# Moving weight conversion, stage A, a fold and an evacuation between the ticks of a Fourier and two-layer-pair kernel

## The chip, the cores and the metric

The kernel runs on one core of one Trainium2 chip. The metric is device time in microseconds (us), median of several executions. Five engines work beside each other, each through its own queue in program order: TensorE (PE; its weight loads are listed as PEld), VectorE (DVE), ScalarE (ACT), GpSimd (POOL) and SyncE (SP, which only issues DMAs). An instruction that waits holds up all that stands behind it in its own queue.

## The reference

```
X   = fft(fft(x, axis=1), axis=2).real        # x: 2 x 3008 x 256
h   = X.reshape(6016, 256) @ w_in             # 256 x 2048
g   = where(h > 0, h, exp(min(h, 0)) - 1)
y   = g @ w_out                               # 2048 x 256
h2  = y @ w2_in
g2  = max(h2, 0) + alpha * min(h2, 0)
out = g2 @ w2_out
```

All four weight matrices arrive as 64 bit floats and are turned into 32 bit floats on the chip.

## The kernel before, in words

**Precision.** A matmul operand is kept as a pair hi + lo of the PE's faster 32 bit type. A product takes three matmuls: w hi by x hi, w lo by x hi, w hi by x lo (`PASSES`, L465). ACT writes hi (a copy that rounds), and POOL or DVE subtracts to get lo.

**Stages.** Stage A is the first transform (L181), stage B the second (L277); the third is folded into w_in (`w_fold`, L376). Then come 96 *ticks* of the first layer pair (L598) and 48 *pairs* of the second (L705). A tick t belongs to one block of 512 (or 452) tokens and one slice f of 128 of the 2048 hidden features. Blocks and slices come in the order of `SEGS` (L42): ticks 0 to 7 are block 0 with f 0 to 7, ticks 8 to 15 block 1 with f 0 to 7, ticks 16 to 23 block 0 with f 8 to 15, ticks 24 to 31 block 1 with f 8 to 15, and from tick 32 on one block each 16 ticks.

**One tick** puts its instructions out in this order: hooks *pre*; gemm1(t) on PE (6 matmuls, L477); pt (L610) and ht (L614) on DVE; hi of tick t-2 on ACT (L589); hooks *mid*; where the segment of t-3 ends, its gemm2 and the evacuation of half of the accumulators by DVE (L513); ReLU and exp on ACT (L630, L636, and from tick 42 on L641 into PSUM); lo of t-2 on POOL (L595); the combination of t-1 on DVE (L582, L579); where a segment ended, the other half of its accumulators by ACT (L511); hooks *end*; and last gemm2(t-3) on PE (12 matmuls, L493). So gemm2(16) is the last thing of tick 19, and gemm2(20) of tick 23. PE is about one tick ahead of ACT and POOL. Segments end so that the evacuations lie in ticks 10, 18, 26, 34, 50, 66 and 82.

**Weights.** A conversion of a matrix part takes an ACT copy (`conv_y`, L338) and three DVE steps (`conv_s`: L356, L358, L360). Then `w_split` (L412) makes hi on ACT (L435) and lo on POOL (L436) for one half of the part: half 0 serves two slices f, half 1 the next two. w_out part 2 serves f 8 to 11, part 3 serves f 12 to 15. The hooks of these are set by tables: `CONV1` (part, tick of the copy, ticks of the three steps, ticks of the two splits), `STAGE_A1` (where the two halves of each chunk of the second batch's stage A stand), `FOLD`, and `KEEP` for the second layer's weights (load, copy; steps at +0, +2, +4). All are registered at L822 to L899. `at_split` puts a split among the *end* hooks of its tick.

**Start.** Before tick 0 stage B of block 0 runs with half a part of w_out converted beside it (L297 to L307): the DVE steps stand between the subtractions that make the low part of stage B's output, which `hold` keeps back and `release` puts out.

The PSUM of gemm1 has four banks that go round; from tick 42 on it has two, and exp takes the other two.

Of the kernel before, what the change touches and what calls it, by code (L numbers as in the profile page):

```python
# [43 lines left out]
E_PSUM = 42  # L44
# [8 lines left out]
CONV1 = [  # L53
    (('i', 1, 2), 8, (8, 9, 11), ()),
    (('i', 1, 3), 11, (12, 13, 14), ()),
    (('o', 1, 2), 14, (14, 15, 16), (17, 18)),
    (('o', 1, 3), 18, (18, 20, 21), (21, 22)),
]

STAGE_A1 = [  # L60
    (0, (7, 'pre'), (8, 'pre')), (1, (9, 'pre'), (11, 'pre')), (2, (12, 'pre'), (14, 'pre')), (3, (16, 'pre'), (17, 'pre')),
]
LOAD_X = {3: 9}
FOLD = {2: (13, 'pre', 0), 3: (15, 'mid', 0)}
LOAD_V = {(0, 2): 12, (1, 0): 24, (1, 1): 24, (1, 2): 24}
STAGE_B = {(0, 1): 5, (0, 2): 22, (1, 2): 32, (1, 0): 36, (1, 1): 40}
LOAD_ZB = {1: 6, 2: 29, 3: 45, 4: 61, 5: 77}
# [2 lines left out]

KEEP = [
    (("i", 2, 0), 31, 34, 81),
    (("o", 2, 0), 36, 39, 84),
    (("i", 2, 1), 45, 48, 88),
    (("o", 2, 1), 52, 55, 92),
    (("i", 2, 2), 59, 61, 95),
# [1 line left out]
]  # L78
FINAL_1 = [(84, "i", 0, 0), (86, "i", 0, 1), (88, "o", 0, 0), (90, "o", 0, 1), (92, "i", 1, 0), (94, "i", 1, 1)]
DIRECT = {("o", 2, 2): 95, ("o", 2, 3): 0}  # L80
PREP_0 = [("x", 62), ("t3", 64, 65), ("t1", 67, 68), ("b11", None, 69), ("t2", 74, 75), ("b21", None, 76), ("t4", 78, 82),
          ("b22", None, 83)]
FIRST = [
# [21 lines left out]
def tile_fft_moe_elu_moe_prelu(  # L105
# [171 lines left out]
    def stage_b(b, g):  # L277
        v = vt.pop((b, g))
        bl = BL[b, g]
        z = big.tile([128, 2, 2, 512], F32R, tag="big", name="zt")  # L280
        for q in range(2):
            p = mmtile()
            for k in range(4 * q, 4 * q + 4):
                o = p.rearrange("p (e k n) -> p e k n", e=2, k=4)[:, :, k % 4, :]
                mm(out=o, lhsT=v[:, k, 0:128], rhs=r64_sb[:, 0:128], start=True, stop=False)
                mm(out=o, lhsT=v[:, k, 128:256], rhs=r64_sb[:, 128:256], start=False, stop=True)
            pv = p.rearrange("p (e m) -> p e m", e=2)
            own = BLOCKS[bl][2] - (MOVED if bl == LONG else 0)
            m = min(256, own - q * 256)
            cuts = [(z, q * 256, 0, m)]  # L290
            if q == 1 and bl == SHORT:
                cuts.append((moved, 0, m, m + MOVED))
            for to, c0, m0, m1 in cuts:
                hi = to[:, 0, :, c0:c0 + m1 - m0]
                act(out=hi, in_=pv[:, :, m0:m1], func=ACTF.Copy)
                hold(("b", b, g, q), tt, out=to[:, 1, :, c0:c0 + m1 - m0], in0=pv[:, :, m0:m1], in1=hi.bitcast(F32), op=ALU.subtract)
            if b == g == 0:  # L297
                if q == 0:
                    release("b", b, g, 0)
                    delta_0(v)  # L300
                    conv_y("o", 1, 0, 0)
                else:
                    spread_0()
                    conv_s("o", 1, 0, 0, 0)
                    release("b", b, g, 1)
                    conv_s("o", 1, 0, 0, 1)
                    conv_s("o", 1, 0, 0, 2)  # L307
        if bl == LONG:
            hold(("b", b, g, 1), nc.gpsimd.tensor_copy, out=z[:, :, :, BLOCKS[bl][2] - MOVED:BLOCKS[bl][2]], in_=moved.bitcast(F32))
        zt[bl] = z  # L310
# [40 lines left out]
    def conv_s(kind, layer, c, i, step):  # L351

        t, y = words((kind, layer, c), i)
        hi, y = t[:, :, 1], y.bitcast(I32)
        if step == 0:
            nc.vector.tensor_scalar(out=hi, in0=hi, scalar1=-(1 << 31), scalar2=None, op0=ALU.bitwise_and)  # L356
        elif step == 1:
            stt(out=hi, in0=t[:, :, 0], scalar=29, in1=hi, op0=ALU.logical_shift_right, op1=ALU.bitwise_or)  # L358
        else:
            stt(out=y, in0=y, scalar=3, in1=hi, op0=ALU.logical_shift_left, op1=ALU.bitwise_or)  # L360
# [8 lines left out]
    def hold(key, fn, *a, **kw):  # L369
        held.setdefault(key, []).append(lambda: fn(*a, **kw))  # L370

    def release(*key):
        for fn in held.pop(key):
            fn()
# [121 lines left out]
    def evac(L, bl, f, first, last, ts, ds=(0, 1)):  # L496
        n = BLOCKS[bl][2]
        ac = accs[L, bl]
        if L == 1 and bl not in xs:
            xs[bl] = big.tile([128, 2, 2, 512], F32, tag="big", name="xs")  # L500
        for t in ts:
            for d in ds:
                if L == 1:
                    o = xs[bl][:, d, t, 0:n]
                else:
                    ot = wk.tile([128, 512], F32, tag="s", name="ot", bufs=4)
                    o = ot[:, 0:n]
                if first > 0:
                    tt(out=o, in0=ac[d][t][:, 0:n], in1=xs[bl][:, d, t, 0:n], op=ALU.add)
                elif t == 1:  # L510
                    act(out=o, in_=ac[d][t][:, 0:n], func=ACTF.Copy)  # L511
                else:
                    nc.vector.tensor_copy(out=o, in_=ac[d][t][:, 0:n])  # L513
                if L == 2:
                    for g, a, c0, m in pieces(bl):
                        nc.sync.dma_start(out=out[d * 128:(d + 1) * 128, c0 + t * BLK_N[g]:c0 + t * BLK_N[g] + m],
                                          in_=o[:, a:a + m])
            if L == 1 and last == NFT - 1 and 1 in ds:
                nc.sync.dma_start(out=xd[bl][:, :, t, 0:n], in_=xs[bl][:, :, t, 0:n])
# [48 lines left out]
    ticks = [(1, bl, f, f0, f1 - 1) for bl, f0, f1 in SEGS for f in range(f0, f1)]  # L568
    NT = len(ticks)
    LAG = 3  # L570

    def parts(t):
        return (slice(0, 1), slice(1, 2)) if t == 0 else (slice(0, 2),)
# [24 lines left out]
    def tick(t, pre, mid, end):  # L598
        cur = ticks[t] if t < NT else None
        for fn in pre:  # L600
            fn()
        if cur:
            L, bl, f = cur[:3]
            n = BLOCKS[bl][2]
            p = gemm1(bl, f, t >= E_PSUM)
            ht = wk.tile([128, 2, 512], F32, tag="h", name="ht")
            et = wk.tile([128, 2, 512], F32, tag="e", name="et", bufs=3)
            st[t] = dict(n=n, f=f, h=ht[:, :, 0:n], e=et[:, :, 0:n])
            pt = wk.tile([128, 512], F32, tag="s", name="pt", bufs=4)
            stt(out=pt[:, 0:n], in0=zb[bl][:, 0:n], scalar=an_sb[:, f:f + 1], in1=p[0], op0=ALU.mult, op1=ALU.add)  # L610
            for i, op in enumerate((ALU.add, ALU.subtract)):
                if t == 1:
                    combine(0, parts(0)[i:i + 1])
                tt(out=ht[:, i, 0:n], in0=pt[:, 0:n], in1=p[1], op=op)  # L614
        if t == 1:
            split_hi(0)
            split_lo(0)
        if t - 2 in st and t > 3:
            split_hi(t - 2)
        for fn in mid:  # L620
            fn()
        over = t < NT and t - LAG in st and ticks[t - LAG][2] == ticks[t - LAG][4]
        if over:
            s = st.pop(t - LAG)
            gemm2(*ticks[t - LAG], s["hi"], s["lo"])
            evac(*ticks[t - LAG], (0,))
        if cur:
            s = st[t]
            for i in parts(t):
                act(out=s["e"][:, i], in_=s["h"][:, i], func=ACTF.Relu, scale=-1.0)  # L630
                if t == 2:
                    combine(1)
                    split_hi(1)
                    split_lo(1)
                if t < E_PSUM or t == NT - 1:
                    act(out=s["e"][:, i], in_=s["e"][:, i], func=ACTF.Exp, scale=-1.0)  # L636
            if E_PSUM <= t < NT - 1:
                s["x"] = []
                for i in range(2):
                    s["x"].append(ps.tile([128, 512], F32, tag="ee", name="eet", bufs=2)[:, 0:s["n"]])  # L640
                    act(out=s["x"][i], in_=s["e"][:, i, :], func=ACTF.Exp, scale=-1.0)  # L641
        if t - 2 in st and t > 3:
            split_lo(t - 2)
        if t - 1 in st and t > 2:
            combine(t - 1)
        if over:
            evac(*ticks[t - LAG], (1,))
        for fn in end:
            fn()
        u = {2: 0, 3: None}.get(t, t - LAG)  # L650
        if u in st and t < NT:
            last_1(u)
# [138 lines left out]
    with tc.manual_schedule():  # L791
# [45 lines left out]
        at(9, load, ("o", 1, 2))  # L837
        for c, (t, where, n) in FOLD.items():
            at(t, w_fold, c, where=where)
# [48 lines left out]
        for bl in range(2, NBLK):  # L888
            for i, (pre, mid) in enumerate(AHEAD):
                for where, todo in (("pre", pre), ("mid", mid)):  # L890
                    for what, *args in todo:
                        at2(bl * NFT // 2 - len(AHEAD) + i, does[what], bl, *args, where=where)
        for name, t, *cs in PREP_0:
            if name == "x":
# [95 lines left out]
```

## Time and profile before

| | |
|---|---|
| median of 3 runs | 959.3 us (958.94 to 959.51) |
| the profiled execution's own time | 959.1 us |
| its span, first to last instruction | 957.3 us |
| mean granted TensorE clock | 0.999 |
| PE busy | 945.2 us, 99% of the span |
| DVE, ACT, POOL busy | 716.1, 654.3, 627.4 us |

The span is what lies between the first and the last instruction of the program; the time is 1.8 us longer. A busy PE counts a matmul from its start to a modelled end, so that short waits between two matmuls can hide in it. In a timeline row the bracket gives the idle time of that engine before the row, and what ended it.

### The profile page before, as it was taken

What the parts mean: (1) busy time and instruction counts of PE and PEld (TensorE: products, weight loads), DVE (VectorE), ACT (ScalarE), POOL (GpSimd) and SP (SyncE); (2) the same over time, 40 slices, a digit from 0 to 9 for tenths busy, and PEclk for the clock granted to TensorE, in tenths of its full rate; (3) what the DMA queues carried; (4) which work ended last, traced back from release to release, by engine and by line L of the source; (5) the groups of instructions that cost most, each with busy time, mean ns of one, the idle gap of its engine ahead of it and who ended that gap; (6) DMA issues with size and microseconds to landing.
All of it is one profiled execution on the core that took longest, in us unless ns stands there. A gap on an engine that the chain in (4) does not pass through costs nothing.

```text
span 957.3 us, 12202 instructions
## 1 busy us (share of the span) xinstructions
PE 945.2 (99%) x4206; PEld 768.5 (80%) x4206; DVE 716.1 (75%) x1015; ACT 654.3 (68%) x915; POOL 627.4 (66%) x495
## 2 busy tenths in 40 slices
PE   9999999999999999999999999999999999999998
PEld 3677678799888877888888888889988888888886
DVE  2899899989999998887787675565666567566564
ACT  5778777767788887888765665656566566565553
POOL 1366578755968779987878855647565664664543
PEclk9999999999999999999999999999999999999999
DMA  8966222311322210130230110020020011001001
GB/s 326 321 187 161 58 78 88 100 49 41 100 84 98 90 45 34 45 110 22 69 130 1 39 45 0 7 83 1 1 73 10 0 45 45 1 1 45 0 1 45
DMA packets 27189, 64.10 MB, mean 67 GB/s; under 512 B 3124, under 2 KB 11572, under 8 KB 25080
## 3 DMA queue, kind: packets, MB, share of 16 engines
q1 hardware_dynamic: 25696, 62.09, 19.6%
q10 hardware_dynamic: 1176, 1.07, 0.3%
q8 instruction: 33, 0.54, 0.2%
q0 software_dynamic: 256, 0.17, 0.1%
q14 instruction: 28, 0.23, 0.1%
HBM read 41.53 MB, written 21.79 MB: 66 GB/s over the span
## 4 chain that ended last, share of the span: by engine, by line
PE 83%; DVE 10%; issue 2%; ACT 2%; POOL 1%; ACTq 0%; DVEq 0%; POOLq 0%
PE acc L493 45%; PE eet L672 13%; PE mmt L672 10%; PE mmt L477 7%; DVE ht L614 2%; DVE et L582 2%; PE eet L477 2%; DVE pt L610 2%; PE mmt L187 1%; DVE w L358 1%; POOL lo L595 1%; DVE et L579 1%; DVE w L360 1%; PE eet L381 1%; ACT et L630 1%
## 5 line engine op out<-in xcount | busy, mean ns | idle before, releaser
L493 PE MATMUL acc<-hi,wo 128*128 128x512 f32 (+1 forms) x1536 | 429.4, 386 | 2.8 <-ACT hi L589 1.5
L698 POOL TENSOR_TENSOR lo<-et,hi 128x512 fp32r<-128x512 f32 (+1 forms) x190 | 237.6, 1281 | 180.8 <-ACT hi L692 180.8
L595 POOL TENSOR_TENSOR lo<-et,hi 128x512 fp32r<-128x512 f32 (+1 forms) x192 | 276.3, 1461 | 94.4 <-ACT hi L589 48.9
L493 PEld LDWEIGHTS acc<-hi,wo 128*128 128x128 f32 x1536 | 287.9, 188 | 59.5 <-ACT xs L511 2.2
L493 PE MATMUL acc<-lo,wo 128*128 128x512 f32 (+1 forms) x768 | 258.4, 387 | 1.0 <-POOL lo L595 1.0
L692 ACT ACTIVATE hi<-et 128x1024 fp32r<-128x1024 f32 (+1 forms) x96 | 100.3, 1045 | 132.2 <-PE acc L493 69.9
L493 PEld LDWEIGHTS acc<-lo,wo 128*128 128x128 f32 x768 | 143.3, 188 | 30.9 <-POOL lo L595 3.9
L630 ACT ACTIVATE et<-ht 128x1024 f32<-128x1024 f32 (+2 forms) x97 | 100.3, 1034 | 64.0 <-DVE ht L614 62.2
L724 DVE TENSOR_TENSOR v<-mmt,p 128x512 f32<-128x512 f32 (+1 forms) x48 | 32.7, 680 | 143.0 <-ACT p L719 142.8
L477 PE MATMUL mmt<-zt,wi 128*128 128x512 f32 (+1 forms) x438 | 113.1, 391 | 0.8 <-DVE ht L614 0.4
L589 ACT ACTIVATE hi<-et 128x1024 fp32r<-128x1024 f32 (+2 forms) x97 | 99.4, 1024 | 5.5 <-DVE et L582 4.1
L614 DVE TENSOR_TENSOR ht<-pt,mmt 128x512 f32<-128x512 f32 (+1 forms) x148 | 93.8, 675 | 8.0 <-DVE pt L610 0.5
L477 PEld LDWEIGHTS mmt<-zt,wi 128*128 128x128 f32 x438 | 81.8, 188 | 19.9 <-issue 1.5
L749 ACT ACTIVATE et<-mmt 128x512 f32<-128x512 f32 (+1 forms) x96 | 55.8, 589 | 28.9 <-PE mmt L672 14.6
L582 DVE SCALAR_TENSOR_TENSOR et<-et,ht 128x1024 f32<-128x1024 f32 (+2 forms) x44 | 67.1, 1525 | 1.4 <-POOL lo L595 1.1
L610 DVE SCALAR_TENSOR_TENSOR pt<-zb,an_sb,mmt 128x512 f32<-128x512 f32 (+1 forms) x72 | 52.7, 731 | 20.0 <-PE mmt L477 19.9
L579 DVE SCALAR_TENSOR_TENSOR et<-eet,ht 128x512 f32<-128x512 f32 (+1 forms) x106 | 67.1, 675 | 0.0
L752 DVE SCALAR_TENSOR_TENSOR et<-et,oma_sb,eet 128x512 f32<-128x512 f32 (+1 forms) x96 | 66.1, 730 | 0.0
L752 DVE SCALAR_TENSOR_TENSOR et<-et,oma_sb,mmt 128x512 f32<-128x512 f32 (+1 forms) x96 | 66.0, 729 | 0.0
L641 ACT ACTIVATE eet<-et 128x512 f32<-128x512 f32 (+1 forms) x106 | 58.9, 588 | 3.7 <-DVE et L579 2.1
L672 PE MATMUL eet<-xo,wi 128*128 128x512 f32 (+1 forms) x216 | 59.8, 385 | 0.0
L672 PE MATMUL mmt<-xo,wi 128*128 128x512 f32 (+1 forms) x216 | 59.8, 385 | 0.0
(123 smaller groups left out, 1249.9 us busy)
## 6 DMA issues: line engine op xcount, KB each, us to landing
w<-w_in SPq DMA_DIRECT2D x8, 1024.0 KB, 9.7
w<-w_out SPq DMA_DIRECT2D x7, 1024.0 KB, 7.7
ud<-uc SPq DMA_DIRECT2D x20, 256.0 KB, 4.2
vt<-ud SPq DMA_DIRECT2D x5, 1024.0 KB, 5.0
xd<-xs SPq DMA_DIRECT2D x10, 512.0 KB, 3.4
xs<-xd SPq DMA_DIRECT2D x5, 1024.0 KB, 4.9
out_t<-ot SPq DMA_DIRECT2D x16, 256.0 KB, 2.2
xc<-x SPq DMA_DIRECT2D x5, 768.0 KB, 11.4
```

Source lines behind the costliest of these rows:

```text
L477: mm(out=p[:, 0:n], lhsT=lhsT, rhs=rhs, start=(i == 0), stop=(i == len(ops) - 1))
L493: mm(out=accs[L, bl][d][t][:, 0:n], lhsT=w[:, a, o, d * 128:(d + 1) * 128], rhs=(hi, lo)[b][:, t, 0:n], start=(f == first and i == 0), sto ...
L579: stt(out=s["e"][:, i, :], in0=s["x"][i], scalar=-1.0, in1=s["h"][:, i, :], op0=ALU.add, op1=ALU.max)
L582: stt(out=s["e"][:, i], in0=s["e"][:, i], scalar=-1.0, in1=s["h"][:, i], op0=ALU.add, op1=ALU.max)
L589: act(out=s["hi"][:, i, 0:s["n"]], in_=s["e"][:, i], func=ACTF.Copy)
L595: nc.gpsimd.tensor_tensor(out=s["lo"][:, i, 0:n], in0=s["e"][:, i, :], in1=s["hi"][:, i, 0:n].bitcast(F32), op=ALU.subtract)
L614: tt(out=ht[:, i, 0:n], in0=pt[:, 0:n], in1=p[1], op=op)
L630: act(out=s["e"][:, i], in_=s["h"][:, i], func=ACTF.Relu, scale=-1.0)
L672: mm(out=bank[:, 0:n], lhsT=w[:, a], rhs=x2[b][:, 0:n], start=(first and m == 0), stop=(last and m == 2), skip_group_check=True)
L692: act(out=s["hi"][f][:, :, 0:n], in_=s["g"][f], func=ACTF.Copy)
L698: eng.tensor_tensor(out=s["lo"][f][:, t, 0:n], in0=s["g"][f][:, t], in1=s["hi"][f][:, t, 0:n].bitcast(F32), op=ALU.subtract)
L752: stt(out=o, in0=o, scalar=oma_sb[:, 2 * j + f:2 * j + f + 1], in1=h, op0=ALU.mult, op1=ALU.add)
```

## The change

```diff
 CONV1 = [
     (('i', 1, 2), 8, (8, 9, 11), ()),
     (('i', 1, 3), 11, (12, 13, 14), ()),
-    (('o', 1, 2), 14, (14, 15, 16), (17, 18)),
-    (('o', 1, 3), 18, (18, 20, 21), (21, 22)),
+    (('o', 1, 2), 15, (15, 16, 17), (18, 19)),
+    (('o', 1, 3), 19, (19, 20, 21), (22, 23)),
 ]
 STAGE_A1 = [
-    ..., (3, (16, 'pre'), (17, 'pre')),
+    ..., (3, (15, 'pre'), (17, 'pre')),
 ]
-FOLD = {2: (13, 'pre', 0), 3: (15, 'mid', 0)}
+FOLD = {2: (13, 'pre', 0), 3: (16, 'pre', 0)}
 KEEP = [
-    (("o", 2, 0), 36, 39, 84),
+    (("o", 2, 0), 34, 37, 84),
-PREP_0 = [..., ("b11", None, 69), ...
+PREP_0 = [..., ("b11", None, 70), ...
@@ stage_b
                     conv_s("o", 1, 0, 0, 0)
+                    conv_s("o", 1, 0, 0, 1)
                     release("b", b, g, 1)
-                    conv_s("o", 1, 0, 0, 1)
                     conv_s("o", 1, 0, 0, 2)
@@ tick
             if E_PSUM <= t < NT - 1:
+                if over:
+                    evac(*ticks[t - LAG], (1,))
                 s["x"] = []
...
-        if over:
+        if over and not E_PSUM <= t < NT - 1:
             evac(*ticks[t - LAG], (1,))
```

The conversion and the splits of w_out's parts 2 and 3 go one tick later (the last two steps of part 3 keep their ticks). The first half of stage A's last chunk goes one tick earlier, and the last fold goes from the middle of tick 15 to the head of tick 16. One part of the second layer's w_out is loaded and converted two ticks earlier. A cast for the second layer (b11) goes one tick later. In ticks 50, 66 and 82 ACT evacuates its half of the accumulators ahead of its exp instead of behind it. In the start, the second conversion step goes ahead of the last subtraction of stage B.

## Rows read from the trace of the kernel before

**Rows 1.** the page's part on engines: busy us (share of the span) x instructions

```profile
PE 945.2 (99%) x4206; PEld 768.5 (80%) x4206; DVE 716.1 (75%) x1015; ACT 654.3 (68%) x915; POOL 627.4 (66%) x495
```

**Rows 2.** what PE waited for, whole span: us in total, times, longest

```profile
PE eet L381 <- DVE w L360: 1.3, 2, 0.9
PE acc L493 <- POOL lo L595: 1.0, 3, 0.5
PE mmt L477 <- DVE zt L370: 0.4, 1, 0.4
PE mmt L235 <- DMA vt<-ud: 0.2, 1, 0.2
```

**Rows 3.** timeline, start: start us, us, engine line operation tiles xcount [idle before <-releaser]

```profile
1.46 3.78 PE L802 MATMUL mmt<-warm 128*128 128x512 f32 x4 [1.46 <-DVE warm L798]
...
32.73 0.69 DVE L370 TENSOR_TENSOR zt<-eet,zt 128x512 fp32r<-128x512 f32 x1 [0.64 <-ACT zt L295]
...
33.34 0.68 DVE L358 SCALAR_TENSOR_TENSOR w<-w 128x512 int32<-128x512 int32 x1
...
34.66 0.74 DVE L610 SCALAR_TENSOR_TENSOR pt<-zb,an_sb,mmt 128x512 f32<-128x512 f32 x1
...
39.28 2.12 PE L493 MATMUL acc<-hi,wo 128*128 128x512 f32 x8 [1.47 <-ACT hi L589]
```

**Rows 4.** timeline, ticks 15 to 20

```profile
110.93 3.70 PE L381 MATMUL eet<-w,c_sb 128*128 128x512 f32 x8 [0.94 <-DVE w L360]
...
123.47 2.29 DVE L360 SCALAR_TENSOR_TENSOR w<-w,w 128x1024 int32<-128x1024 int32 x1
...
128.87 1.52 PE L477 MATMUL mmt<-zt,wi 128*128 128x512 f32 x6
...
130.66 1.31 POOL L436 TENSOR_TENSOR wo<-w,wo 128x512 fp32r<-128x512 f32 x1 [0.48 <-ACT wo L435]
...
134.31 0.62 PE L493 MATMUL acc<-hi,wo 128*128 128x512 f32 x2
...
135.56 0.63 ACT L435 ACTIVATE wo<-w 128x512 fp32r<-128x512 f32 x1
...
136.27 1.30 POOL L436 TENSOR_TENSOR wo<-w,wo 128x512 fp32r<-128x512 f32 x1 [0.81 <-ACT wo L435]
...
141.11 0.73 PE L493 MATMUL acc<-lo,wo 128*128 128x512 f32 x2 [0.29 <-POOL lo L595]
```

**Rows 5.** timeline, ticks 21 to 23

```profile
149.36 1.21 DVE L360 SCALAR_TENSOR_TENSOR w<-w,w 128x1024 int32<-128x1024 int32 x1
...
155.34 1.98 PE L493 MATMUL acc<-hi,wo 128*128 128x512 f32 x8
...
156.80 1.29 POOL L436 TENSOR_TENSOR wo<-w,wo 128x512 fp32r<-128x512 f32 x1
```

**Rows 6.** timeline, ticks 39 to 43

```profile
233.64 0.68 DVE L356 TENSOR_SCALAR w<-w 128x1024 int32<-128x1024 int32 x1
...
234.52 0.68 DVE L610 SCALAR_TENSOR_TENSOR pt<-zb,an_sb,eet 128x452 f32<-128x452 f32 x1 [0.20 <-PE eet L477]
...
241.91 2.19 DVE L358 SCALAR_TENSOR_TENSOR w<-w 128x1024 int32<-128x1024 int32 x1
...
246.01 0.88 PE L477 MATMUL mmt<-zt,wi 128*128 128x452 f32 x3 [0.36 <-DVE ht L614]
```

**Rows 7.** timeline, ticks 66 to 72

```profile
343.77 1.14 ACT L641 ACTIVATE eet<-et 128x512 f32<-128x512 f32 x2 [0.74 <-DVE et L579]
...
344.84 1.06 ACT L511 ACTIVATE xs<-acc 128x512 f32<-128x512 f32 x2
...
345.47 0.73 PE L493 MATMUL acc<-hi,wo 128*128 128x512 f32 x2 [1.19 <-ACT xs L511]
...
365.11 2.54 POOL L595 TENSOR_TENSOR lo<-et,hi 128x512 fp32r<-128x512 f32 x2
...
367.70 0.73 PE L493 MATMUL acc<-lo,wo 128*128 128x512 f32 x2 [0.52 <-POOL lo L595]
```

More of the change, by code (lines that the diff above doesn't have):

```diff
@@ L55 @@
     (('i', 1, 3), 11, (12, 13, 14), ()),
-    (('o', 1, 2), 14, (14, 15, 16), (17, 18)),
-    (('o', 1, 3), 18, (18, 20, 21), (21, 22)),
+    (('o', 1, 2), 15, (15, 16, 17), (18, 19)),
+    (('o', 1, 3), 19, (19, 20, 21), (22, 23)),
 ]
 STAGE_A1 = [
-    (0, (7, 'pre'), (8, 'pre')), (1, (9, 'pre'), (11, 'pre')), (2, (12, 'pre'), (14, 'pre')), (3, (16, 'pre'), (17, 'pre')),
+    (0, (7, 'pre'), (8, 'pre')), (1, (9, 'pre'), (11, 'pre')), (2, (12, 'pre'), (14, 'pre')), (3, (15, 'pre'), (17, 'pre')),
 ]
 LOAD_X = {3: 9}
-FOLD = {2: (13, 'pre', 0), 3: (15, 'mid', 0)}
+FOLD = {2: (13, 'pre', 0), 3: (16, 'pre', 0)}
 LOAD_V = {(0, 2): 12, (1, 0): 24, (1, 1): 24, (1, 2): 24}
@@ L80 @@
 DIRECT = {("o", 2, 2): 95, ("o", 2, 3): 0}
-PREP_0 = [("x", 62), ("t3", 64, 65), ("t1", 67, 68), ("b11", None, 69), ("t2", 74, 75), ("b21", None, 76), ("t4", 78, 82),
+PREP_0 = [("x", 62), ("t3", 64, 65), ("t1", 67, 68), ("b11", None, 70), ("t2", 74, 75), ("b21", None, 76), ("t4", 78, 82),
           ("b22", None, 83)]
```

## Prediction

> **What bounds the kernel now.** The page's part on engines comes first: PE is busy 945.2 us, 99% of the span [rows 1]. The total is therefore PE's work, which the change leaves alone, and the few places where PE waits. The list of PE's waits comes next, and it is short: the waits that the change can touch add up to a handful of microseconds [rows 2]. The timeline around each of them tells what arrives last there. At 39.28 PE waits 1.47 us for the first block's chain through DVE and ACT [rows 3]; at 110.93 the last fold waits 0.94 us for a conversion step on DVE, at 141.11 PE waits for a lo from POOL [rows 4]; at 246.01 it waits 0.36 us for ht [rows 6]; at 345.47 it waits 1.19 us for ACT's evacuation, and at 367.70 0.52 us for POOL [rows 7]. The last thing to read is what just comes in time today: the weight halves that ACT and POOL make at the end of a tick, beside the gemm2 that reads them [rows 4, 5]. That is where this change bites.
>
> **The change part by part.** Plus is slower. I count against the profiled execution's own 959.1 us (span 957.3); the median of the runs, 959.3, is 0.2 above it.
>
> *Start.* DVE stands idle 0.64 us before the last subtraction of stage B at 32.73; the conversion step that runs behind it takes 0.68 us [rows 3]. Put ahead, it fills that hole, and what is queued behind (pt at 34.66, then the chain to PE's wait at 39.28) comes up to 0.6 us earlier. The subtraction itself ends about where it does now, so PE's third matmul is not held up. A part may be lost at tick 4, where PE meets a DMA that it already waits 0.2 us for, but the wait of 0.4 us for stage B's bank at tick 6 [rows 2] hangs on the same DVE chain and gives that back. Ends 0 and -0.6; I take -0.5.
>
> *Fold at the head of tick 16, stage A in tick 15.* The matmuls are the same, in another order: stage A, gemm1(15) and gemm2(12) now stand ahead of the fold, several microseconds of work, so the conversion that ends at 110.9 is long done. What goes is 0.94 us and the restart of a matmul. ACT does stage A's copies ahead of hi(13); its reader, gemm2(13), stands behind the fold (3.70 us) and gemm1(16) (1.52 us, as the one at 128.87), and these cover it [rows 4]. Ends -0.9 and -1.4; I take -1.1.
>
> *First half of w_out part 2, one tick later.* Half 0 is now split at the end of tick 17: POOL has it at 130.66 + 1.31 = 131.97. The reader is gemm2(16), the last work of tick 19, at 134.31, and its second matmul (about 0.25 us on) takes the lo [rows 4]. There are 2.6 us to spare. After the change half 0 stands at the end of tick 18, just where half 1 stands today: ACT at 135.56, behind its half of the evacuation, POOL at 136.27 to 137.57 [rows 4]. Today's PE would have to wait 3.0 us for it, and the new PE comes 1.1 us earlier, at about 133.5. The late end is 137.57, if DVE does not get ahead. The early end takes off PE's 1.1 us and the 0.63 us of the ACT copy that leaves tick 17: 135.84. The wait is thus 2.4 to 4.1 us, part for hi from ACT and, after one matmul, the rest for lo from POOL. What decides is whether DVE has tick 18's pt out earlier; it now carries the third step at the end of tick 17, 2.29 us at 123.47 when POOL runs beside it, 1.21 us at 149.36 when not [rows 4, 5]. I go near the late end: +3.5. In exchange POOL does lo(17) behind this and PE comes later, so that the wait at 141.11 goes: 0.29 us on PE and as much again of restart, -0.5 (ends -0.3, -0.7).
>
> The Trainium skill (SBUF — State Buffer, Who interferes with whom) says that a DVE instruction with two SBUF inputs and a GpSimd instruction that reads SBUF exclude each other, and the later one stands still. By that rule the third step costs 2.29 us, and the wait goes to its late end, with a sum 0.6 us above mine; the two rows of that step agree with it.
>
> *First half of part 3, one tick later.* The reader is gemm2(20) at 155.34, its second matmul at 155.6. Half 0 moves to the end of tick 22, where half 1's lo ends today at 156.80 + 1.29 = 158.09 [rows 5]. That is 2.5 us late; POOL's queue comes up by at most the 0.6 us of the ACT copy that leaves tick 21, hence 1.9, and 1.5 if POOL runs freer. I take +2.0. The second halves keep a tick of room: they are read one gemm2 after the next.
>
> *Second layer's w_out part, two ticks earlier.* Its step at tick 37 puts 0.68 us of DVE work ahead of tick 38; at tick 39 the second step takes the first one's place, 0.5 us more at 1.21 us, 1.5 more at 2.19; there are 0.20 us of slack at 234.52. So DVE is about 1.0 us later at tick 40. At tick 41 the third step (1.21 to 2.3 us) replaces the second (2.19 us at 241.91). PE's wait at 246.01 therefore grows by about 0.8 us; it ends between -0.6 (gone, if the third step runs alone) and +2.0 [rows 6]. What leaves tick 43 came after the wait. The load on SP goes ahead of a store; it has whole ticks to land.
>
> *ACT's evacuation ahead of exp.* At tick 66 ACT is idle 0.74 us before exp at 343.77, and the evacuation follows at 344.84 [rows 7]. Put ahead, it starts where that idle time begins, 343.03; the wait goes, 1.19 us and the restart, -1.3, since PE needs the copy at 345.47 - 1.3 = 344.2 and its first half takes 0.5 us. Exp comes 0.3 us later, which fits in that hole. But POOL decides the next wait: it is busy without a break up to 365.11 + 2.54 = 367.65, and PE goes on at 367.70 [rows 7]. PE comes there earlier and waits longer. The cast moved to tick 70 stands in the same POOL queue ahead of that lo, so it changes the order and not the end. ACT's hi comes up to half a microsecond sooner, so not all is given back: 0.7 of 1.3. Net -0.6 (ends 0, -1.4). At ticks 50 and 82 the list shows no such wait, and nothing changes.
>
> Sum: -0.5 - 1.1 + 3.5 - 0.5 + 2.0 + 0.8 - 0.6 = **+3.6 us**, 962.7 us.
>
> **The rivals.**
> *The halves come at their early ends.* If DVE keeps step with PE at tick 18, the two waits are 2.4 and 1.5, tick 43 stays as it is and tick 66 keeps 0.9: -0.5 - 1.1 + 2.4 - 0.5 + 1.5 - 0.9 = +0.9, 960.0 us. For it: DVE loses 1.7 us of work from tick 18. Against it: the order of ACT's queue, with the evacuation ahead of the split [rows 4].
> *PE does not wait for the halves (faster).* If ACT starts the split at the end of tick 18 before about 132.0, that is 3.5 us ahead of the row at 135.56, POOL is done in time, and both new waits are nothing. The price is then -0.5 - 1.1 - 0.6 with tick 43 as it is, less 0.5 at 141.11: -2.7, 956.4 us. It decides at the gemm2 of tick 19. Against it: tick 18's ReLU, exp and two copies stand ahead on ACT.
> *The pause is long enough for PE's clock to fall.* The start shows the price: four matmuls take 3.78 us there [rows 3], eight of the same form 3.70 us at 110.93 [rows 4]. A stretch of PE work as long as those first 5 us, done at half speed, costs some 2.6 us more: 965.3 us. Against it: with today's waits, of up to 1.47 us, the mean granted clock is 0.999. The Trainium skill (TensorE: Matmul & The Clock Gate, HAM oscillation — how this bites in real kernels) warns that a pause between bursts can put the clock back to its lower level; no row here has a pause of 3 us in mid kernel, so the trace doesn't decide.
> *The evacuation does not free PE.* If ACT's queue or the DVE ahead of tick 66 is the real limit, -0.6 becomes 0: 963.3 us.
>
> **How the numbers follow.** Forecast 0.60, early ends 0.17, no wait 0.08, clock 0.09, no gain at tick 66 0.06. A measurement of this kernel can tell 0.2% from no change, which is 1.9 us: 957.4 to 961.2. Of the forecast, whose own range is 960.7 to 964.8 by the ends of its terms, nearly all is slower, a little is same; the early ends are mostly same. Slower 0.74, same 0.19, faster 0.07. The range goes from 959.0, which takes in most of the early ends, to 965.5, which takes in the clock.
>
> **What would show it.** In tick 19 the first gemm2 waits over 2 us, first on ACT's wo (L435), one matmul later on POOL's wo (L436); in tick 23 the same with 1.5 to 2.5 us; no wait ahead of the fold; none on ACT's xs at tick 66, and a longer one on POOL some six ticks later; a longer wait for ht at tick 43; gemm2(0) about 0.5 us earlier. The prediction is wrong if wo (L435, L436) is not among PE's releasers, or if PE waits there and the time still does not rise because later waits shrink by as much.

## The result, and the profile after

| | time, us | profiled execution / span, us | PE busy, us | mean granted clock |
|---|---|---|---|---|
| before | 959.19 (958.91 to 959.59, 6 runs) | 959.1 / 957.3 | 945.2 | 0.999 |
| after | 966.14 (965.28 to 967.03, 6 runs) | 966.41 / 964.6 | 948.6 | 0.996 |

The ratio is 1.0072 (95%: 1.0059 to 1.0085): 7 us slower, nearly twice the 3.6 us forecast, and just over the upper end of the range (965.5).

The page after is read first. Against [rows 1], PE has the same 4206 instructions and 3.4 us more of busy time. Waits alone would have left that as it was. The clock's row names the place: the sixth of 40 slices, 121 to 145 us, where PE's row dips too.

```profile
PE 948.6 (98%) x4206; PEld 770.2 (80%) x4206; DVE 715.5 (74%) x1015; ACT 654.7 (68%) x915; POOL 622.7 (65%) x495
...
PE   9999989999999999999999999999999999999998
...
PEclk9999989999999999999999999999999999999999
```

What PE waited for, after (total, times, longest), answering to [rows 2]: ACT's and POOL's wo are new at the top, the long wait of a fold for w (L360) is gone, and so is the one for ACT's xs (1.2 us before, in a line that Rows 2 doesn't show).

```profile
PE acc L493 <- ACT wo L435: 2.9, 2, 2.6
...
PE acc L493 <- POOL wo L436: 1.4, 2, 0.8
...
PE mmt L477 <- DVE ht L614: 1.1, 3, 0.4
PE acc L493 <- POOL lo L595: 1.0, 2, 0.5
PE mmt L477 <- DVE pt L610: 0.7, 1, 0.7
```

DVE's timeline at the start, and PE's at the last fold, answer to [rows 3] and the first of [rows 4]. The pt comes at 34.20 instead of 34.66; the fold, now behind tick 15's work, waits for nothing.

```profile
34.20 0.75 DVE L610 SCALAR_TENSOR_TENSOR pt<-zb,an_sb,mmt 128x512 f32<-128x512 f32 x1
...
113.85 3.59 PE L381 MATMUL mmt<-w,c_sb 128*128 128x512 f32 x8
```

The timeline of PE after, tick 18 to tick 20, answering to [rows 4]. The row at 127.20 is the one at 128.87 before; the rows from 135.44 on are gemm2(16), which began at 134.31. PE stands still for 2.63 us, then for 0.57. Behind that two matmuls take 0.86 us from start to start (137.81 to 138.67), twice the 0.45 of a pair of the same form before (x2 at 134.31).

```profile
127.20 1.52 PE L477 MATMUL mmt<-zt,wi 128*128 128x512 f32 x6
...
131.28 1.52 PE L477 MATMUL eet<-zt,wi 128*128 128x512 f32 x6
135.44 0.79 PE L493 MATMUL acc<-hi,wo 128*128 128x512 f32 x1 [2.63 <-ACT wo L435]
136.80 0.80 PE L493 MATMUL acc<-hi,wo 128*128 128x512 f32 x1 [0.57 <-POOL wo L436]
137.39 0.63 PE L493 MATMUL acc<-lo,wo 128*128 128x512 f32 x1
137.81 1.06 PE L493 MATMUL acc<-hi,wo 128*128 128x512 f32 x2
138.67 0.63 PE L493 MATMUL acc<-lo,wo 128*128 128x512 f32 x1
...
141.66 1.62 PE L477 MATMUL mmt<-zt,wi 128*128 128x512 f32 x6
```

The same stretch by windows (busy us of PE, PEld, DVE, ACT, POOL; granted clock; DMA). The clock goes from its upper level (1.0, 2.4 GHz) to the lower one (0.5, 1.2 GHz) while PE stands still: by the share of 0.74 in the window from 134 at about 135.0, 2.2 us after PE's last matmul ended (131.28 + 1.52 = 132.80) and before the second pause. It is back in the window from 142.

```profile
132.00:134.00 2.00, 0.80 (x4) 0.34 (x2) 2.00 (x4) 1.97 (x3) 0.12 (x1) 1.00 0.48 201
134.00:136.00 2.00, 0.56 (x1) 0.29 (x1) 1.90 (x4) 2.00 (x4) 0.54 (x1) 0.74 0.00 0
136.00:138.00 2.00, 1.43 (x4) 1.02 (x4) 2.00 (x3) 2.00 (x3) 2.00 (x2) 0.50 0.00 0
138.00:140.00 2.00, 2.00 (x7) 1.54 (x6) 1.53 (x1) 1.89 (x3) 2.00 (x2) 0.50 0.00 0
140.00:142.00 2.00, 2.00 (x7) 1.58 (x6) 0.00 (x0) 0.53 (x1) 1.90 (x2) 0.55 0.00 0
142.00:144.00 2.00, 2.00 (x10) 1.65 (x9) 0.90 (x2) 0.53 (x1) 1.34 (x2) 1.00 0.00 0
```

PE's other rows after, in ticks 23, 43 and 66 to 73 ([rows 5 to 7]). The row at 155.34 is now at 159.93 with a wait for each of ACT's and POOL's halves. The one wait at 246.01 has become two, at 251.45 and 252.72. The wait at 345.47 is gone, but two for ht come (one is shown), and the one for lo at 367.70 has become two.

```profile
159.93 0.50 PE L493 MATMUL acc<-hi,wo 128*128 128x512 f32 x1 [0.24 <-ACT wo L435]
161.28 1.90 PE L493 MATMUL acc<-hi,wo 128*128 128x512 f32 x7 [0.85 <-POOL wo L436]
...
251.45 0.89 PE L477 MATMUL mmt<-zt,wi 128*128 128x452 f32 x3 [0.67 <-DVE pt L610]
252.72 0.89 PE L477 MATMUL mmt<-zt,wi 128*128 128x452 f32 x3 [0.38 <-DVE ht L614]
...
348.92 0.98 PE L477 MATMUL mmt<-zt,wi 128*128 128x512 f32 x3 [0.32 <-DVE ht L614]
...
373.81 0.73 PE L493 MATMUL acc<-lo,wo 128*128 128x512 f32 x2 [0.46 <-POOL lo L595]
375.04 0.73 PE L493 MATMUL acc<-lo,wo 128*128 128x512 f32 x2 [0.50 <-POOL lo L595]
```

The balance comes from one measure: how much later gemm1's first matmul starts in each tick than it did before. Two such differences can be read from the rows: the start of tick 18, 127.20 - 128.87 = -1.67, and, behind the last of the waits, the matmuls that wait for lo in tick 72, 375.04 - 367.70 = +7.34. What changes from tick to tick is the price of a place; the last column is the difference behind it:

| place | forecast, us | measured, us | offset behind it |
|---|---|---|---|
| start | -0.5 | -0.45 | -0.45 |
| fold, stage A | -1.1 | -1.22 | -1.67 |
| tick 19, first half of part 2 | +3.5 | +6.30 | +4.63 |
| lo at 141.11 | -0.5 | -0.46 | +4.17 |
| tick 23, first half of part 3 | +2.0 | +1.72, then -0.24 | +5.65 |
| second layer's w_out part, tick 43 | +0.8 | +1.06 | +6.71 |
| evacuation ahead of exp | -0.6 | +0.63 | +7.34 |
| sum | +3.6 | +7.34 | |

Tick 19's 6.30 are 2.79 and 1.14 of start-to-start excess at the two waits, 3.9, and 2.4 for the matmuls behind them that come some 0.43 us apart instead of 0.227.

### The profile page after: what moved, and what is told of

It is laid out like the page before. It is cut to its first block, busy times and chain, and to the rows that moved or that the text cites. A ratio compares the mean times of both kernels' runs of the same rounds, so it can differ in the third digit from the quotient of the medians.

```text
span 964.6 us, 12198 instructions
## 1 busy us (share of the span) xinstructions
PE 948.6 (98%) x4206; PEld 770.2 (80%) x4206; DVE 715.5 (74%) x1015; ACT 654.7 (68%) x915; POOL 622.7 (65%) x495
## 4 chain that ended last, share of the span: by engine, by line
PE 83%; DVE 10%; issue 2%; ACT 2%; POOL 1%; DMA 1%; SPq 0%; ACTq 0%; DVEq 0%; POOLq 0%
PE acc L493 46%; PE eet L674 13%; PE mmt L674 10%; PE mmt L477 7%; DVE ht L614 2%; DVE et L582 2%; PE eet L477 2%; DVE pt L610 2%; DVE w L358 1%; PE mmt L187 1%; DVE w L360 1%; PE mmt L381 1%; DMA xc<-x 1%; ACT et L630 1%; POOL lo L595 1%
## 5 line engine op out<-in xcount | busy, mean ns | idle before, releaser
L477 PE MATMUL mmt<-zt,wi 128*128 128x512 f32 (+1 forms) x432 | 112.6, 392 | 2.0 <-DVE ht L614 1.1
L477 PEld LDWEIGHTS mmt<-zt,wi 128*128 128x128 f32 x432 | 80.4, 188 | 22.4 <-DVE ht L614 3.1
```

What stands on the lines that cost most here:

```text
L477: mm(out=p[:, 0:n], lhsT=lhsT, rhs=rhs, start=(i == 0), stop=(i == len(ops) - 1))
```

## The experiments

The theory after this comparison was that the two late first halves cost their waits, that the first wait is long enough to drop PE's clock, and that the second layer's part and the evacuation cost about 1.0 and 0.6 us. Each ratio is to the kernel before, timed beside it, with its 95% interval in brackets. A clock that is called 1.0 is that of the one run with a trace.

**The splits alone back.** In the changed kernel:

```diff
-    (('o', 1, 2), 15, (15, 16, 17), (18, 19)),
-    (('o', 1, 3), 19, (19, 20, 21), (22, 23)),
+    (('o', 1, 2), 15, (15, 16, 17), (17, 18)),
+    (('o', 1, 3), 19, (19, 20, 21), (21, 22)),
```

> The changed kernel, but the second step (the split into hi and lo) of both halves of w_out parts 2 and 3 is back at the ends of ticks 17 and 18, 21 and 22; load, first and third steps stay a tick late. Theory (the late first halves cost PE two waits, 3.9 us in tick 19 and 1.7 us in tick 23, and the first of them also costs 2.2 us at half clock): PE finds both halves ready, the clock stays at 1.0, and 966.1 falls by 6.3 and 1.7; the wait of 0.5 us for lo at 141 may come back: 959 us (958.5 to 960). Rival (it is the later load and first step that make the halves late, whatever tick the split stands in): PE still waits for wo, and the time stays over 962 us.

Measured 960.42 us, ratio 1.0013 (1.0004 to 1.0022): 5.7 us of the loss gone. PE waits for no wo and the clock is 1.0, so the rival falls. The time is 0.4 above the theory's range, and gemm1's starts show where: 0.85 us goes in tick 19, where PE now waits for ACT's half of the evacuation (0.24 us at 134.26), and 0.44 in tick 20, where it waits for POOL's lo (0.73 us at 140.57; five such waits and 2.0 us in all, three and 1.0 before, [rows 2]).

**Both rows wholly back.** The two lines are as in the kernel before.

> The changed kernel with both rows of the w_out table (parts 2 and 3: load, steps and splits) as they were before; start, fold and stage A, the second layer's w_out part, the cast b11 and the evacuation stay changed. Theory (offsets of PE's first matmuls by tick): -0.5 at the start, -1.2 at the fold, +1.0 at tick 43, +0.6 from tick 66 to 73, which is -0.1 on 959.2: 959.1 us (958.4 to 959.8), the same as with the splits alone put back. Rival (the loss is in the moves of the second half of the run, which the late conversion only comes on top of): over 961 us.

Measured 959.42 us, 1.0002 (0.9993 to 1.0010), inside the theory's range; the rival falls. Against the kernel above, the later load and steps by themselves cost 1.0 us. The four moves that are left sum to nothing: start and fold gain what the other two lose.

**The first half of part 2 alone back.** In the changed kernel:

```diff
-    (('o', 1, 2), 15, (15, 16, 17), (18, 19)),
+    (('o', 1, 2), 15, (15, 16, 17), (17, 19)),
```

> The changed kernel, but the second step of the first half of w_out part 2 is back at the end of tick 17 (the second half stays in tick 19, part 3 stays late). Theory (this one split costs the wait of 3.9 us and the 2.2 us at half clock): no wait for wo in tick 19, clock at 1.0, 6.1 us less: 960 us (959.5 to 961.5; a second wait may come, as the second half at the end of tick 19 is read in tick 20). Rival (both halves are late, as the whole chain of load and steps is): the wait only moves to the second half in tick 20, with 2 us and more: 963 us or over.

Measured 962.37 us, 1.0039 (1.0026 to 1.0053): between the two, and neither was right. There is no wait for wo in ticks 19 and 20 and the clock stays 1.0, so tick 19 costs 0.8 (again with a wait for ACT's evacuation) instead of 6.3 us. But POOL now has no break from 135.91 to 149, and in tick 21 PE waits for its lo, which costs 1.1. Two of the five runs, without a trace, are slower than the rest, 963.61 and 963.66 us, with mean clocks of 0.997 and 0.998. POOL's rows, then PE's:

```profile
135.91 4.09 POOL L595 TENSOR_TENSOR lo<-et,hi 128x512 fp32r<-128x512 f32 x2 [0.81 <-POOL lo L595]
...
141.21 8.02 POOL L595 TENSOR_TENSOR lo<-et,hi 128x512 fp32r<-128x512 f32 x4
```

```profile
145.82 0.72 PE L493 MATMUL acc<-lo,wo 128*128 128x512 f32 x2 [0.86 <-POOL lo L595]
```

**The pause filled.** The changed kernel with 16 matmuls added in gemm2(16), whose results are overwritten:

```diff
-        for t, d, i in order:
+        for k, (t, d, i) in enumerate(order):
+            if L == 1 and bl == 0 and f == 8 and k < 2:
+                for _ in range((11, 5)[k]):
+                    mm(out=accs[L, bl][k][0][:, 0:n], lhsT=wi[1, 0][:, 0, 0, 0:128], rhs=zt[0][:, 0, 0, 0:n],
+                       start=True, stop=True)
```

> The changed kernel with 16 added matmuls in tick 19 whose results nobody reads (11 ahead of the first matmul of gemm2(16), 5 ahead of its second), so that PE works through the wait that it has there; weights and loads come as late as in the changed kernel. Theory (PE's clock falls to half for 6.8 us because PE had stood idle for 2.6 and then 0.6 us; this costs 2.2 us): the granted clock stays at 1.0 from 134 to 143, the ten to eleven matmuls behind the wait go at 0.23 instead of 0.43 us, and 966.1 becomes 964 us (963.4 to 964.6). Rival (the clock falls for another reason, or the matmuls are slow because the weights or the port are late): the clock row of that stretch still shows half speed and the time is 966 us or more, up to 967 if the added matmuls run past the end of the wait.

Measured 963.79 us (963.66 to 964.20), 1.0049 (1.0037 to 1.0062): 2.35 us less than the changed kernel, with 16 matmuls more. PE's timeline and a window in it: the real matmuls still start at 135.15 and 136.64, as late as the weights make them (135.44 and 136.80 in the changed kernel), but behind them all goes at 0.227 us and the clock is 1.0.

```profile
132.37 2.65 PE L494 MATMUL acc<-zt,wi 128*128 128x512 f32 x11
135.15 0.50 PE L497 MATMUL acc<-hi,wo 128*128 128x512 f32 x1
135.49 1.32 PE L494 MATMUL acc<-zt,wi 128*128 128x512 f32 x5
136.64 0.40 PE L497 MATMUL acc<-hi,wo 128*128 128x512 f32 x1
...
139.15 1.52 PE L477 MATMUL mmt<-zt,wi 128*128 128x512 f32 x6
```

```profile
138.00:140.00 2.00, 2.00 (x10) 1.66 (x9) 1.27 (x1) 1.97 (x4) 2.00 (x2) 1.00 0.00 0
```

So the slow matmuls come from PE's standing still, not from late weights or a busy port. Their price is 2.35 us, of which up to 0.16 is the second wait's earlier end (136.64 against 136.80).

**Half of the pause filled.** The same lines with six matmuls, ahead of the first one only.

> The changed kernel with 6 added matmuls, whose results nobody reads, ahead of gemm2(16) only: they fill 1.4 of the 2.6 us in which PE stood idle, and leave a pause of 1.2 us and the second one of 0.6 us as they were. Theory (it takes the whole pause to drop the clock; before, PE's pauses of 1.2 to 1.5 us left it at 1.0): clock 1.0, time 963.8 us as with the filled pause (963.4 to 964.2). Rival (the two shorter pauses still drop it): half speed from 136 to 143, 966.1 us.

Measured 964.33 us (963.82 to 965.65), 1.0055 (1.0042 to 1.0068), 0.1 above the theory's range. In the trace PE stands still for 1.27 and 0.86 us and the clock stays at 1.0 through the stretch; the window that holds the end of the second pause and the matmuls behind it:

```profile
136.00:138.00 2.00, 1.40 (x6) 1.18 (x7) 2.00 (x2) 2.00 (x3) 2.00 (x2) 1.00 0.00 0
```

Four of the five runs are at 963.8 to 964.4 with a mean clock of 0.999 or 1.0; the fifth is at 965.65 with 0.998. It has no trace, so that the shorter pauses never drop the clock is not shown.

**The late rows alone**, on the kernel before, where PE comes to tick 19 1.65 us later than in the changed kernel:

```diff
-    (('o', 1, 2), 14, (14, 15, 16), (17, 18)),
-    (('o', 1, 3), 18, (18, 20, 21), (21, 22)),
+    (('o', 1, 2), 15, (15, 16, 17), (18, 19)),
+    (('o', 1, 3), 19, (19, 20, 21), (22, 23)),
```

> The kernel before with one move only: both rows of the w_out table (parts 2 and 3) a tick later, as in the changed kernel; PE comes to tick 19 1.65 us later than there. Theory (the halves end at a time of ACT's and POOL's own, so PE's gain at start and fold is simply waited away): the wait of tick 19 is 3.9 - 1.65 = 2.25 us, that of tick 23 still 1.7, that at 141 goes (-0.5), and with a pause of only some 1 us the clock stays at 1.0: 962.6 us (962 to 963.2). Rival (any pause for the weights here drops the clock): 2.2 more, 964.8 us. Rival (ACT's and POOL's halves come later by the same 1.65 us, as they hang on PE): the whole price again, 966.1 + 1.65 - 0.6 - 0.4 = 966.8 us.

Measured 965.93 us, 1.0070 (1.0056 to 1.0084). The theory that the halves come at a time of their own falls; the second rival is right, though 0.9 too high. In its trace PE comes to tick 18 at 129.54 instead of 127.20 (0.7 of the difference is from the first ticks), and waits as long:

```profile
129.54 1.52 PE L477 MATMUL mmt<-zt,wi 128*128 128x512 f32 x6
...
137.77 0.49 PE L493 MATMUL acc<-hi,wo 128*128 128x512 f32 x1 [2.63 <-ACT wo L435]
139.13 0.79 PE L493 MATMUL acc<-hi,wo 128*128 128x512 f32 x1 [0.86 <-POOL wo L436]
```

The chain of the changed kernel, read back from 135.38, says why (start, us, what): it leaves PE with gemm1(17) (L477) and runs through DVE's work of tick 17, the third step (L360), pt and ht of tick 18, and ACT's et and xs to wo. It hangs on PE's own earlier work, and shifts with it. Each row is a step of the chain:

```profile
123.26 0.72 PE eet L477 x3
...
127.36 2.24 DVE w L360
129.60 0.67 DVE pt L610
...
131.74 1.07 ACT et L630
...
133.80 1.07 ACT xs L511 x2
134.87 0.52 ACT wo L435
```

**Only the splits late**, so that the third step leaves that chain. In the changed kernel:

```diff
-    (('o', 1, 2), 15, (15, 16, 17), (18, 19)),
+    (('o', 1, 2), 14, (14, 15, 16), (18, 19)),
```

> The changed kernel, but of w_out part 2 only the two splits stay a tick late (ends of ticks 18 and 19): load and three steps are back at ticks 14, 14, 15 and 16, so that the third step is not on DVE at the end of tick 17. Theory (the chain that the pause of 2.6 us hangs on runs from PE's gemm1(18) over the third step, 2.32 us on DVE, pt and ht of tick 18, ACT's ReLU, exp and two copies to the split; without the third step it is some 1.4 to 2 us shorter): PE stands idle for 0.7 to 1.3 us before gemm2(16) and 0.6 to 0.9 us for the low half, the clock stays at 1.0, and 966.1 loses 1.4 to 2.0 and 2.2: 962 us (961.5 to 962.8). Rival (the split's place in ACT's queue alone makes the wait, whatever DVE does): the pause stays over 2 us, half speed behind it, 965.5 to 966.5 us.

Measured 962.54 us, 1.0037 (1.0023 to 1.0050): inside the theory's range, and the rival falls. DVE's pt of tick 18 starts 0.88 us behind gemm1(18) (127.10), not 2.32 us as in the changed kernel (127.20 to 129.52). Those 1.44 us are what the pause is shorter by, 2.63 to 1.20, and the clock stays up: its mean is 1.0, and the matmuls behind go at 0.23 us. One of the five runs, without a trace, is at 963.94 us with 0.998.

```profile
127.98 0.75 DVE L610 SCALAR_TENSOR_TENSOR pt<-zb,an_sb,mmt 128x512 f32<-128x512 f32 x1 [0.73 <-PE mmt L477]
...
133.91 0.50 PE L493 MATMUL acc<-hi,wo 128*128 128x512 f32 x1 [1.20 <-ACT wo L435]
135.27 0.50 PE L493 MATMUL acc<-hi,wo 128*128 128x512 f32 x1 [0.86 <-POOL wo L436]
```

The split's place alone costs 962.54 - 959.42 = 3.1 us with part 3's 1.5 in it; load and steps a tick late, with the clock that they take along, another 3.6.

**Start, fold and stage A alone**, on the kernel before: the edits of `stage_b`, `STAGE_A1` and `FOLD`.

> The kernel before with only the moves of the start (conversion step ahead of the last subtraction) and of the fold and stage A of ticks 15 and 16. Theory (what PE gains there is not given back, as no engine but PE is near its limit from tick 20 on): -0.5 - 1.2, and perhaps the wait at 141 stays: 957.5 us (957 to 958). Rival (PE comes earlier to the chains of DVE and POOL at ticks 43 and 66 to 73, and waits there for as much longer): 958.7 to 959.2 us.

Measured 957.65 us (957.40 to 958.17), 0.9984 (0.9975 to 0.9993). This one beats both kernels: -0.6 at the start and -1.2 at the fold, of which 0.35 goes again at tick 25 and nothing later.

**The second layer's part alone**, on the kernel before (`KEEP`: 36, 39 to 34, 37).

> The kernel before with one move only: the second layer's w_out part 0 two ticks earlier (load 34, steps to 37). Theory (the steps at ticks 39 and 41 make DVE late for ticks 42 and 43): PE's waits for pt and ht near 246 us grow from 0.36 to 1.05 us together, +1.0: 960.2 us (959.8 to 960.6). Rival (DVE is late there only because stage B and the conversions ahead of it were moved as well): no change, 959.2 us.

Measured 960.28 us, 1.0016 (1.0007 to 1.0025): the theory's number. DVE's third step, 2.19 us, now stands ahead of the pt that PE needs at 245.97, as in the changed kernel. One of the eleven runs took 963.80 us at a mean clock of 1.0, so a single slow run need not be the clock's. DVE's row, then PE's:

```profile
243.13 2.19 DVE L360 SCALAR_TENSOR_TENSOR w<-w,w 128x1024 int32<-128x1024 int32 x1
```

```profile
245.97 0.88 PE L477 MATMUL mmt<-zt,wi 128*128 128x452 f32 x3 [0.70 <-DVE pt L610]
```

**The evacuation alone**, on the kernel before (the edits of `tick`).

> The kernel before with one move only: at ticks 50, 66 and 82 ACT's evacuation stands ahead of exp (the cast b11 stays in tick 69). Theory (in the changed kernel PE gains 1.2 us at the first matmul of tick 68, as it no longer waits for ACT, and gives back 1.8 by tick 73 through waits for ht and for lo; the give-back comes from ACT's changed order, not from the cast): the same offsets here, -1.2 at tick 68 and +0.6 from tick 73 on: 959.8 us (959.4 to 960.2). Rival (the cast b11, moved to tick 70, is what makes the second wait for lo; the evacuation by itself keeps its gain): -1.2 at tick 68, of which 0.5 to 1.2 stays: 958.2 to 958.7 us.

Measured 959.57 us, 1.0004 (0.9995 to 1.0013). In its trace PE is 1.45 us earlier at tick 68 and 0.2 later from tick 73 on. That the gain is given back is shown; that a loss remains is not, as the interval holds 1. DVE's row, and then POOL's, show the place: ACT's hi comes 0.8 us sooner, POOL starts its pair of lo at 346.18 and not 346.99, and DVE's subtraction of xs takes 1.78 us instead of 1.41.

```profile
347.49 1.78 DVE L548 TENSOR_TENSOR xs<-xs 128x512 f32<-128x512 f32 x1
```

```profile
346.18 2.54 POOL L595 TENSOR_TENSOR lo<-et,hi 128x512 fp32r<-128x512 f32 x2 [2.64 <-ACT hi L589]
```

Half of POOL's pair is 1.27 us. The subtraction, issued at 347.49, is done 0.55 us behind the end of the second lo (346.18 + 2.54 = 348.72); before, issued at 347.43, it was done 0.58 us behind the end of the first (346.99 + 1.27 = 348.26, if that lo took as long). In both it looks as if DVE stood until the lo ahead of it was through; no run was made to test this.

**Evacuation and cast b11**, on the kernel before (`PREP_0`: 69 to 70 as well).

> The kernel before with two moves: ACT's evacuation ahead of exp, and the cast b11 in tick 70 instead of 69. Theory (evacuation sets the sign, the cast little): 959.8 us (959.4 to 960.2), as with the evacuation alone, two waits for lo of 0.5 us near tick 72. Rival (the two belong together: without the cast in tick 69 POOL is free sooner, and the pair gains): 958 to 958.6 us, with no more than one wait for lo.

Measured 959.74 us, 1.0007 (0.9998 to 1.0016). Two waits for lo, 0.41 and 0.50 us, at 366.96 and 368.19: the pair does not gain, and the cast decides nothing that these runs can tell.

**Part 3 late**, on the kernel with start, fold and stage A.

> The kernel with only the moves of start, fold and stage A (957.65 us), and the w_out row of part 3 a tick later. Theory (part 3's first half costs two waits in tick 23, 0.4 and 1.1 to 1.3 us, and no clock): 957.65 + 1.7 = 959.35 us (958.9 to 959.8). Rival (the wait in tick 23 is an echo of the late part 2, whose POOL work runs into it): no wait there, 957.7 us.

Measured 958.59 us, 0.9994 (0.9986 to 1.0003). The waits are there (0.31 us for ACT's half, 0.85 for POOL's, tick 23) and cost 1.7 us at tick 24, so they are no echo of part 2. By the end 0.94 is left: 0.23 comes back by tick 31 and 0.34 at tick 68, which the theory, 0.8 too high, had left out.

## Why the prediction was wrong

**The step that failed** is the rival that was set aside: "Against it: with today's waits, of up to 1.47 us, the mean granted clock is 0.999", with a chance of 0.09. The sum put the clock at nothing, and it cost 2.4 us. The rival had the mechanism right, and its price came close (2.6 us; 2.35 by the filled pause). That is luck in part: the price was taken from the start, where the clock reads 1.0 in the trace although the four matmuls take twice as long, and the low stretch was 6.8 us here, with PE standing still in some of it. The argument against the rival compared a pause of over 3 us with pauses of half that length, which can't speak against it. With the clock in, the same sum would have given 965.3. The forecast of a long wait and a chance of 0.09 for the clock did not go together, as no row spoke against it. The Trainium skill (TensorE: Matmul & The Clock Gate, HAM oscillation — how this bites in real kernels) was cited there with its warning that a pause between bursts can put the clock to its lower level. The traces agree for a first pause of 2.63 us, and show the clock at 1.0 behind pauses of 1.27 and 0.86, and of 1.20 and 0.86 us.

**The second failure** is the evacuation: -0.6 forecast, +0.63 measured in the changed kernel, +0.2 alone, which is within the noise. The sum looked at ACT and POOL behind tick 66, and not at DVE, which only a rival named. By the windows of the trace before, DVE is busy for 9.99 of the 10.20 us from 341.80 to 352.00:

```profile
341.80:352.00 10.20, 8.97 (x39) 6.97 (x39) 9.99 (x16) 8.74 (x12) 6.62 (x6) 1.00 0.27 103
```

PE's wait for ACT only hid that DVE's ht would be late; taking it away put PE in front of that. Behind that, the subtraction beside the earlier lo took 0.37 us longer. The Trainium skill (SBUF — State Buffer, Who interferes with whom) says that a DVE instruction with two SBUF inputs contends with a GpSimd instruction that reads SBUF; the 1.41 and 1.78 us fit this, but no run here tests it.

**The sizes.** Start, fold and the wait at 141 were right within 0.12 us. The wait of tick 19 was 3.9, not 3.5; the reason given (the third step ahead of tick 18's pt) is the one that the kernel with only the splits late shows. What the prediction had wrong is the time from which it measured. Near its late end it took the halves to come at today's times and PE's gain to be lost in the wait; and it let PE come 1.1 us earlier, without the 0.5 of its own start term (1.67 measured). The late rows alone show that the halves hang on PE, so the gain was not lost and the wait was that long by itself. The prices add: 966.14, without 1.06 for the second layer's part and 0.63 for the evacuation, and with the 1.67 of start and fold given up, is 966.1; the late rows alone took 965.93. Part 3 cost 1.7, and 1.5 behind its give-back, not 2.0; the second layer's part 1.06, not 0.8, as its third step took 2.18 us, near the long end. The range is too narrow for its own terms: their ends add up to -0.8 and +7.4, 958.3 to 966.5 us, where the prediction writes 960.7 to 964.8 and doesn't say why the terms should not all err one way.

Of the 3.7 us between the forecast and the traced run (+3.6 and +7.34), 2.4 are the clock, 1.2 the evacuation, 0.4 the wait and 0.3 the second layer's part, less 0.5 for part 3.

## What to carry to other kernels

When a forecast contains a pause of TensorE, decide in the same breath what the matmuls behind the pause cost at the lower clock; that shorter pauses left the clock up says nothing of a longer one. A wait that is taken away is worth only what the next-busiest engine leaves: read the windows of every engine over the next ticks, not only of those that the moved instruction stands on. And before counting a late transfer or split in absolute time, follow its chain back: if it starts at the waiting engine itself, as here, coming earlier neither shortens nor lengthens the wait.

## What the runs showed of the hardware

The stretch at the lower clock is not always as long. In the changed kernel's trace it lasts from about 135.0 to 141.8 us, and the matmuls behind the waits lose 2.4 us to it. In the trace of the late rows alone, behind a first pause of the same 2.63 us, it lasts from about 138.8 to 142.2, and they lose 1.6. Two windows of that trace:

```profile
138.00:139.00 1.00, 0.27 (x1) 0.00 (x0) 1.00 (x2) 1.00 (x2) 1.00 (x1) 0.90 0.00 0
139.00:140.00 1.00, 0.87 (x2) 0.78 (x3) 1.00 (x1) 1.00 (x2) 1.00 (x2) 0.50 0.00 0
```

The changed kernel's six runs fall into two groups that would fit such lengths: three with a mean granted clock of 0.998 take 965.28 to 965.87 us, three with 0.996 take 966.41 to 967.03. Only one of them, at 0.996, has a trace, so that this makes the spread is likely but not shown.

The mean granted clock of a whole run must be read with care. In the trace of the kernel before, PE's last matmul ends at 953.2 us and the clock falls to 0.5 at 955.8. This alone makes the mean 0.999, and it costs nothing; single runs of that kernel read 0.998 to 1.0.
